# A fifth block product in sevenths: M7 of the first product, for token groups 3 to 6, and the last difference of G's parts on GpSimd

## The chip, the cores and the metric

The kernel runs on one core of a Trainium2 chip. The core has a matrix engine (TensorE, in the profile PE, with its weight loads as PEld), a vector engine (VectorE, DVE), a scalar engine (ScalarE, ACT), GpSimd (POOL) and SyncE (SP), which issues most of the DMAs. Each engine takes its own instructions in the order in which the program has them, and waits on semaphores for the others. The metric is the device time of one execution in microseconds (us), as the median of several runs; one further execution is recorded instruction by instruction, and that is the profile.

## The reference: what is computed

```python
# q, k, v: (4, 8, 768, 64); centroids: (8, 16, 64); w_in: (512, 2048); w_out: (2048, 512); all float32
mask = q_assign[:, :, :, None] == k_assign[:, :, None, :]      # nearest centroid, queries and keys
scores = np.where(mask, scale * np.matmul(q, k.transpose(0, 1, 3, 2)), -1000000000.0)
attn = softmax(scores);  attn_out = np.matmul(attn, v)
x = attn_out.transpose(0, 2, 1, 3).reshape(B * S, H * D)       # 3072 tokens x 512
h = x @ w_in                                                   # the first product
g = np.where(h > 0.0, h, np.exp(np.minimum(h, 0.0)) - 1.0)     # ELU
out = g @ w_out                                                # the second product
```

Only the two products behind the attention concern us, and of these the first one for the last four of six token groups.

## The kernel before

**Groups and blocks.** The 3072 tokens go in six groups of 512 (`k_` 0 to 5 in the code, groups 1 to 6 in this text). For each group the kernel computes the first product, transposed (2048 rows of h on the partitions, 512 tokens along them), applies ELU, and leaves the result in the buffer `g` (the tile `kq_g`); then it computes the second product from `g` and stores 512 rows of the output. All of it is float32.

**Seven block products.** Both products are cut by Winograd's form of Strassen's scheme. The weights are quartered into a11, a12, a21, a22 and the group's x into x11, x12, x21, x22; s1 to s4 and t1 to t4 are sums of these quarters. Seven products M1 = a11 x11, M2 = a12 x21, M3 = s4 x22, M4 = a22 t4, M5 = s1 t1, M6 = s2 t2, M7 = s3 t3 take the place of eight, and with U2 = M1 + M6 and U4 = U2 + M5 the quarters of h are c11 = M1 + M2, c12 = U4 + M3, c21 = U2 + M7 - M4 (the minus is in t4), c22 = U2 + M7 + M5.

**Two ways to do one of the seven.** A block product is 1024 rows by 256 tokens, with 256 to sum over. *By fourths*: the rows come in four parts (`u` 0 to 3); each part is one `block_product` (line 794), four matmuls of 128 x 128 weights with 256 columns, into one PSUM bank of 512. *In sevenths*: the same scheme is applied once more inside the block, and the block is one *unit* of seven small products m1 to m7, each of four matmuls with 128 columns. The class `InUnit` (line 1159) does that for the first product, `OutUnit` for the second. The small weight sums of a unit, where they are not blocks of the weights themselves, lie in DRAM (`far_in`) and are streamed in by SyncE, ten slots ahead (`fetch`, `weights`, `stream_of`).

**Which product is done how.** Group 1 and 2 do all seven of the first product by fourths (`unit`). In groups 3 to 6 (`FIRST_IN` = 2) the first product of a group has two stages. The first is the chain of four units M1, M6, M5, M2 (`IN_UNITS`), which runs behind the seven `OutUnit`s of the previous group's second product, in one chain (`chain`, line 1246). The second stage is `rest_of_group` (line 1326): M3, M7 and M4 by fourths, with three block products for each `u`, added in PSUM to what the chain left in `g`.

**The chain's own order.** For each unit u the chain issues m6, m2, m1 of the next unit, m7, m5 of the next unit, m3, m4; the last unit has no next one, and so only five products. A unit works in a set of four banks; two sets (`sets`) alternate from unit to unit. Between the products, ScalarE copies m1 into the bank of m6 (line 1223), m5 out to SBUF (1227), bank 2 to bank 3 (1265) and bank 3 out to SBUF (1281), and VectorE adds these in: `b2 += m5` (line 1272) must be done before m3 is accumulated into bank 2, `b4 += u3` (1284) before bank 4 is used. The four results of a unit, one per bank, are taken up by `take` (line 1198): for M1 by copies to c11, for M6 as c21 = U2, for M5 as c12 = U4 with a copy of M5 itself to c22 (line 1207, ScalarE), for M2 by adding c11 in the bank (line 1209). Results 0 and 1 are taken within the unit; 2 and 3 when the next unit's m6 has been issued, or, for the last unit, around its own m3 and at its end. The small sums of x (`xt`, line 1195) are made by GpSimd.

**ELU.** `elu_exp` (line 808) is an exponential on ScalarE from the bank into `g` (810) and a clamp on GpSimd in `g` (811); `elu` (line 813) is one VectorE instruction on `g` and the bank (814).

**The fourths.** For each `u`, `rest_of_group` does s3 t3 into bank b3, which ScalarE had filled with c21 = U2 from `g` (`begin_rest`, line 1323); VectorE makes c22 as b3 + M5 (line 1341); s4 x22 is added to b2, which had been filled with c12 = U4; a22 t4 is added to b3. Each of the three gets its ELU. Last, VectorE replaces c12 by c22 - c12 (line 1364), one of the differences that the second product needs of G's parts, one `u` later (`behind`, `flush_all`). At the head of the stage stand the four ELUs of c11 (`ready`, from the banks of the unit M2), in the order of banks 2, 0, 1, 3: all four exponentials before anything else on ScalarE, all four VectorE parts after the first block product.

**Tables in group 2.** While group 2's first product runs by fourths, VectorE makes the weight sums for the streams, four instructions to a block (`table_block` for w_out, `in_table_steps` for w_in), in steps that `fill_table` hands out two at a time; SyncE stores them (`keep_far`). The sums s2, s3, s4 of w_in were made by GpSimd in group 1 (`w_step`), and stored by GpSimd's DMAs into `s2_far` and `w_far`.

Of the kernel before, what the change touches and what calls it, by code (L numbers as in the profile page):

```python
# [9 lines left out]
F32 = mybir.dt.float32  # L10
# [9 lines left out]
P = 128  # L20
# [41 lines left out]
def main_path(ctx, tc, c, q, k, v, centroids, moe_w_in, moe_w_out, out):  # L62
# [675 lines left out]
    def x_parts(k_):  # L738
        a, b_ = slice(GS * k_, GS * k_ + QS), slice(GS * k_ + QS, GS * (k_ + 1))
        return X[:, :2, a], X[:, :2, b_], X[:, 2:, a], X[:, 2:, b_]  # L740
# [18 lines left out]
    w_far = [[far.tile([P, 512], F32, name=f"w_far{u}{n}") for n in range(2)] for u in range(4)]  # L759
    s2_far = far.tile([P, 2, 2, 512], F32, name="s2_far")  # L760

    def w_far_of(u, n):

        if n == 0:
            return s2_far[:, u // 2, :, ts(u % 2, QS)]
        return w_far[u][n - 1].rearrange("p (c n) -> p c n", c=2)

    def w_step(k_, u, n):

# [36 lines left out]
    def as_part(bank, part):  # L806
        return bank.rearrange("p (f n) -> p f n", f=part.shape[1])
# [134 lines left out]
    def table_block(a, at):  # L942


        s3, s2, s4 = (x.rearrange("p (f m) -> p f m", m=P) for x in at)
        q11, q12, q21, q22 = (part_w(a, i, j) for i in range(2) for j in range(2))
        nc.vector.tensor_tensor(s3, q11, q21, op=Alu.subtract)
        yield
        nc.vector.tensor_tensor(q21, q21, q22, op=Alu.add)
        keep_far()  # L950
        yield
        nc.vector.tensor_tensor(s2, q21, q11, op=Alu.subtract)
        yield
# [16 lines left out]
    def thirds(x):  # L970
        return [x[:, ts(m, 512)] for m in range(3)]
# [14 lines left out]
    def table_last(n):  # L986
# [9 lines left out]
        if n == 1:  # L996
            parts = [("s3", s3), ("s2", s2), ("s4", s4)]
            here["a22"].update(parts)
            made.extend((flat_far("a22", x), y) for x, y in parts)

    def table_rest():
        for n in range(4):
            nc.sync.dma_start(dead[n], s2_far[:, n // 2, n % 2])
        for a, at in (
            ("s4", thirds(s_all)),
            ("a11", thirds(p_out)),
            ("a12", thirds(s_all)),
        ):
            yield from table_block(a, at)
        yield from in_table_steps()  # L1010
# [12 lines left out]
    far_in = {  # L1023
        (a, x): far.tile([P, 512], F32, name=f"far_in_{a}_{x}")
        for _, a in IN_UNITS
        for x in (("s1", "s2", "s3", "s4") if a == "s2" else ("s2", "s3", "s4"))
    }
    for i, j, x in ((0, 0, "q11"), (0, 1, "q12"), (1, 1, "q22")):
        far_in["s2", x] = s2_far[:, i, j]

    def in_table_steps():

        for a, s1, at in (
            ("s2", dead[2], p_out),
            ("a11", dead[0], s_all),
            ("s1", dead[0], p_out),
            ("a12", dead[0], s_all),
        ):
            s3, s2, s4 = thirds(at)
            if a == "s2":  # L1040
                q11, q12, q21, q22 = dead
            else:
                q11, q12, q21, q22 = (part_in(a, i, j) for i in range(2) for j in range(2))
            nc.vector.tensor_tensor(s3, q11, q21, op=Alu.subtract)
            yield
            nc.vector.tensor_tensor(s1, q21, q22, op=Alu.add)
            keep_far()
            yield
            nc.vector.tensor_tensor(s2, s1, q11, op=Alu.subtract)
            yield  # L1050
            nc.vector.tensor_tensor(s4, q12, s2, op=Alu.subtract)
            made.extend((far_in[a, x], y) for x, y in (("s3", s3), ("s2", s2), ("s4", s4)))
            if a == "s2":
                made.append((far_in[a, "s1"], s1))
            yield
        keep_far()

    def in_place(n):
        a = ("a11", "s1", "a12")[n]
# [98 lines left out]
    class InUnit:  # L1158
        of, width = "in", 512

        def __init__(self, k_, n):
            self.k_, self.n, self.a = k_, n, IN_UNITS[n][1]
            x11, _, x21, _ = x_parts(k_)
            self.b = (x11, x_s[1], x_s[0], x21)[n]
            self.banks = banks_of(k_, n)
# [31 lines left out]
        def take(self, q_):  # L1197
            bank = self.banks[q_]
            c11, c12, c21, c22 = (part_g(b, q_ // 2, q_ % 2) for b in ("b11", "b12", "b21", "b22"))
            b = as_part(bank, c11)  # L1200
            if self.n == 0:
                nc.scalar.copy(c11, b)
            elif self.n == 1:
                nc.vector.tensor_tensor(c21, b, c11, op=Alu.add)
            elif self.n == 2:
                nc.vector.tensor_tensor(c12, b, c21, op=Alu.add)
                nc.scalar.copy(c22, b)
            else:
                nc.vector.tensor_tensor(b, b, c11, op=Alu.add)

# [3 lines left out]
        def note(self, at):  # L1214
            if at == "m4" and self.n == 2:
                rest_load(1)
            elif at == "m7" and self.n == 3:
                for n in (2, 1):
                    begin_rest(self.k_, 0, n)

    def seven_first(u):
        u.product("m1")
# [82 lines left out]
            u.take(2)  # L1305
            u.taken()

    REST = [(1, 2), (0, 3)]

    def rest_places(u):  # L1310

        return [w_tmp[:, n] if n < 3 else o_rest for n in REST[u % 2]]

    def rest_load(u):
        for n, place in enumerate(rest_places(u)):
            nc.sync.dma_start(place, w_far_of(u, n + 1))

    def begin_rest(k_, u, n):

        part = g[:, 2 * u : 2 * u + 2, QS:]  # L1320
        if n == 2:
            part = g[:, FC // 2 + 2 * u : FC // 2 + 2 * u + 2, :QS]
        nc.scalar.copy(as_part(sets[(k_ + u) % 2][n], part), part)
# [114 lines left out]

    def w_sums(k_):
        for n in range(3):  # L1440
            if n or k_ < FIRST_IN:
                w_step(k_, 0, n)

    def next_group(k_):
# [122 lines left out]
            scale_x(last_n, e_of)  # L1567
    second_product_first(early_on)

    table = table_rest()  # L1570

    def fill_table():
        next(table, None)
        next(table, None)

    for k_ in range(1, N // GS):
        if k_ < FIRST_IN:
# [269 lines left out]
```

## Time and profile before

| | us |
|---|---|
| median of 3 runs (lowest, highest) | 889.41 (888.82, 889.57) |
| the profiled execution: its own time | 889.5 |
| its span, first to last instruction | 887.7 |
| attention and group 1's first product | 0 to about 382 |
| group 1's second product | about 382 to 429.5 |
| group 2's first product | 429.5 to 478 |
| group 2's second product, with the first unit of group 3 begun in it | 478 to about 522 |
| group 3: last of the chain's units ends, and the fourths begin | 547.34 |
| group 3: the fourths end, and the second product begins | 568.06 |
| group 4, 5, 6: the fourths begin | 637.1, 726.9, 816.7 |
| TensorE, VectorE, ScalarE, GpSimd busy | 876.6, 710.7, 447.0, 227.3 |

The span is what the trace covers; the run's own time has 1.8 us more around it. In the trace, TensorE's float32 matmuls come as two records each, so that one small product of four matmuls is "x8". The duration shown for a matmul is modelled and overlaps the next one; the start times give the real pace. For VectorE and ScalarE too, the next instruction starts a little before the one ahead has ended, so a queue's pace is read from its starts. In the timeline, the bracket at the end of a line gives how long the engine was idle before and which instruction ended that.

### The profile page before, as it was taken

The numbers are of one execution on the slowest core, as the hardware profiler recorded it, in microseconds if no ns is written. First come the engines' busy times: TensorE is split into PE (matmuls) and PEld (weight loads), VectorE is DVE, ScalarE is ACT, GpSimd is POOL, SyncE is SP. The second block draws the span as 40 slices with busy tenths as digits, with TensorE's granted clock in tenths as the row PEclk, the third lists the DMA queues.
The fourth block names the chain that finished last, engine by engine and source line by source line (L and its number), as shares of the span: only waits on it lengthen the run. The fifth ranks groups of instructions, "written<-read, shape, count | busy, mean of one in ns | idle before, by whom it ended". The sixth has DMA issues, their size and how long they took to land.

```text
span 887.7 us, 17035 instructions
## 1 busy us (share of the span) xinstructions
PE 876.6 (99%) x6437; PEld 677.6 (76%) x6441; DVE 710.7 (80%) x1041; ACT 447.0 (50%) x853; POOL 227.3 (26%) x293
## 2 busy tenths in 40 slices
PE   8999999999999999999999999999999999999997
PEld 5444444444444448899989999999999999999997
DVE  4789998999988997897688957884788568956784
ACT  6667786787868754412243235422642364225421
POOL 0011121121113555841323013511351035102300
PEclk9999999999999999999999999999999999999999
DMA  7766685366337441165677876286618661876172
GB/s 219 185 127 175 158 181 121 123 125 159 84 107 217 129 141 62 59 148 151 206 249 245 276 212 178 52 279 207 188 48 265 217 191 42 267 205 205 49 231 82
DMA packets 157369, 145.68 MB, mean 164 GB/s; under 512 B 89824, under 2 KB 109280, under 8 KB 156256
## 3 DMA queue, kind: packets, MB, share of 16 engines
q1 hardware_dynamic: 151584, 132.45, 51.0%
q0 software_dynamic: 5408, 11.54, 5.7%
q8 instruction: 53, 0.87, 0.4%
q10 hardware_dynamic: 288, 0.52, 0.2%
q14 instruction: 36, 0.29, 0.1%
HBM read 114.59 MB, written 21.50 MB: 153 GB/s over the span
## 4 chain that ended last, share of the span: by engine, by line
PE 92%; POOL 3%; issue 2%; DVE 1%; DMA 1%; ACT 0%; SPq 0%; POOLq 0%; ACTq 0%
PE bank L1087 23%; PE o_bank L548 15%; PE banks L510 14%; PE bank L797 12%; PE bank L1177 9%; PE o_bank L1087 4%; PE banks L523 3%; PE o_bank L797 2%; PE d_bank L1087 2%; PE o_bank L1177 2%; PE d_bank L568 1%; PE d_bank L438 1%; POOL kq_g L811 1%; PE d_bank L1177 1%; PE banks L616 1%
## 5 line engine op out<-in xcount | busy, mean ns | idle before, releaser
L532 ACT ACTIVATE p_out<-banks 128x768 f32<-128x768 f32 x192 | 154.1, 811 | 25.2 <-PE banks L523 24.2
L548 PE MATMUL o_bank<-p_out,kq_g 128*64 128x384 f32 x768 | 130.9, 490 | 0.7 <-DMA kq_g<-in_v_dram 0.7
L548 PEld LDWEIGHTS o_bank<-p_out,kq_g 128*64 128x64 f32 x768 | 52.3, 137 | 75.5 <-issue 69.8
L811 POOL TENSOR_SCALAR kq_g<-kq_g 128x512 f32<-128x512 f32 x96 | 69.0, 728 | 109.7 <-ACT kq_g L810 108.3
L535 DVE TENSOR_TENSOR sums_w<-p_out 128x1536 f32<-128x1536 f32 x32 | 59.1, 1846 | 10.1 <-ACT p_out L532 10.1
L810 ACT ACTIVATE kq_g<-bank 128x512 f32<-128x512 f32 x68 | 39.8, 602 | 38.5 <-PE bank L797 18.4
L797 PE MATMUL bank<-xT,spare 128*128 128x256 f32 x256 | 59.2, 379 | 0.0
L540 DVE TENSOR_TENSOR sums_w<-sums_w,p_out 128x1536 f32<-128x1536 f32 x32 | 56.2, 1757 | 3.3 <-DVE sums_w L535 0.5
L609 POOL DMA_DIRECT2D sums_w<-xT x28 | 17.7, 649 | 154.3 <-DVE xT L585 92.0
L1087 PE MATMUL bank<-w_out,kq_g 128*128 128x128 f32 x448 | 56.0, 275 | 0.3 <-DVE kq_g L814 0.3
L1087 PEld LDWEIGHTS bank<-w_out,kq_g 128*128 128x128 f32 x448 | 53.4, 192 | 0.8 <-DVE kq_g L814 0.5
L797 PEld LDWEIGHTS bank<-xT,spare 128*128 128x128 f32 x256 | 48.3, 190 | 6.4
L797 PE MATMUL bank<-x_sum,w_in 128*128 128x256 f32 x224 | 52.9, 379 | 0.0
L814 DVE SCALAR_TENSOR_TENSOR kq_g<-kq_g,bank 128x512 f32<-128x512 f32 x68 | 44.9, 679 | 7.7 <-POOL kq_g L811 7.7
L797 PEld LDWEIGHTS bank<-x_sum,w_in 128*128 128x128 f32 x224 | 42.6, 190 | 5.8
L1195 POOL TENSOR_TENSOR spare<-x_sum 128x128 f32<-128x128 f32 x16 | 7.3, 457 | 154.4 <-PE bank L1177 88.8
L1391 DVE TENSOR_TENSOR kq_g<-kq_g 128x1024 f32<-128x1024 f32 x36 | 43.8, 1219 | 0.0
L562 ACT ACTIVATE xT<-o_bank 128x384 f32<-128x384 f32 x32 | 15.6, 489 | 53.8 <-PE o_bank L548 53.8
L604 POOL TENSOR_TENSOR xT<-xT,sums_w 128x384 f32<-128x384 f32 x32 | 41.1, 1305 | 1.6 <-DMA sums_w<-xT 1.6
L510 PE MATMUL banks<-x_sum,xT 64*128 64x384 f32 x192 | 39.8, 492 | 0.0
L510 PE MATMUL banks<-kq_g,xT 64*128 64x384 f32 x192 | 39.6, 491 | 0.0
L510 PE MATMUL banks<-x_sum,kq_g 64*128 64x384 f32 x192 | 39.6, 491 | 0.0
(379 smaller groups left out, 2026.6 us busy)
## 6 DMA issues: line engine op xcount, KB each, us to landing
kq_g<-in_v_dram SPq DMA_DIRECT2D x32, 384.0 KB, 3.7
sums_w<-far_s_s SPq DMA_DIRECT2D x42, 256.0 KB, 3.7
spare<-w_far SPq DMA_DIRECT2D x32, 256.0 KB, 3.0
words_w<-far_s_s SPq DMA_DIRECT2D x26, 256.0 KB, 3.2
out_dram<-p_out SPq DMA_DIRECT2D x22, 256.0 KB, 3.3
w_out<-in_q_dram SPq DMA_DIRECT2D x112, 48.0 KB, 2.6
sums_w<-xT POOLq DMA_DIRECT2D x28, 192.0 KB, 3.2
sums_w<-far_s_q SPq DMA_DIRECT2D x21, 256.0 KB, 3.6
```

Of the source, the lines that this page charges most:

```text
L510: nc.tensor.matmul(s[:, e, :HS], lhsT=kT[b % 2][pr][rows, ts(kt, P)], rhs=qT[half][pr][rows], start=True, stop=False,)
L532: nc.scalar.activation(probs[kt], s[:, :, :HS], Act.Exp, scale=SCALE)
L535: nc.vector.tensor_tensor(add_to, probs_all[:, : 4 * HS], probs_all[:, 4 * HS : 8 * HS], op=Alu.add)
L540: nc.vector.tensor_tensor(add_to, add_to, probs_all[:, 8 * HS :], op=Alu.add)
L548: nc.tensor.matmul(o_bank[64 * e : 64 * e + 64, :HS], lhsT=v_raw[n % 2][:, e, kt], rhs=probs[kt][:, e], start=(kt == 0), stop=(kt == NT - 1),)
L604: nc.gpsimd.tensor_tensor(x_of(n), x_of(n), r, op=Alu.mult)
L797: nc.tensor.matmul(bank[:, ts(f, QS)], lhsT=left[:, ch, ts(f, P)], rhs=right[:, ch], start=first and f == 0 and ch == 0, stop=ch == 1, ski ...
L811: nc.gpsimd.tensor_scalar(to, to, 1.0, 0.0, op0=Alu.min, op1=Alu.max)
L814: nc.vector.scalar_tensor_tensor(to, to, -1.0, as_part(bank, to), op0=Alu.add, op1=Alu.max)
L1087: nc.tensor.matmul(bank[:, :P], lhsT=left[:, f], rhs=right[:, f], start=first and f == 0, stop=last and f == 3, skip_group_check=True,)
L1177: nc.tensor.matmul(bank[:, ts(f, P)], lhsT=left[:, ts(f, P)], rhs=right, start=m in ("m1", "m5") and f == 0, stop=True, skip_group_check=True,
L1391: nc.vector.tensor_tensor(b[to][:, f], b[x][:, f], b[y][:, f], op=op)
```

## The change

In groups 3 to 6, M7 moves from the fourths into the chain, as a fifth unit between M5 and M2. Its four results are taken by two VectorE instructions each: c21 = U2 + M7 in `g`, and c22 = M7 + U4 in the bank. c22 gets its ELU from that bank, in steps that `note` puts behind products of the units M7 and M2 (`fourths`); M5 is no longer copied to c22. The first two fills of b2 and b3 for the fourths (`begin_rest`) move into the same steps. The fourths keep two block products for each `u`, s4 x22 and a22 t4. The difference c22 - c12 goes from VectorE to GpSimd. The set of banks for each unit is renumbered, since the chain has twelve units now instead of eleven.

The s3 sums of w_in get one array in DRAM, `s3_far`, in the form that `s2_far` has, and a table of their own: in group 2, VectorE makes four more sums (block "s3"), SyncE loads four pieces of `s3_far` for them and stores four results. The table's blocks are put in another order, and `fill_table` hands out three steps in each of its first four calls. Of the weight sums for the fourths, s4 alone is loaded.

```diff
-    IN_UNITS = [("M1", "a11"), ("M6", "s2"), ("M5", "s1"), ("M2", "a12")]
+    IN_UNITS = [("M1", "a11"), ("M6", "s2"), ("M5", "s1"), ("M7", "s3"), ("M2", "a12")]
...
     def banks_of(k_, n):
-        return sets[(k_ + n) % 2]
+        return sets[(min(k_, 1) + n) % 2]
...
             elif self.n == 2:
                 nc.vector.tensor_tensor(c12, b, c21, op=Alu.add)
-                nc.scalar.copy(c22, b)
+            elif self.n == 3:
+                nc.vector.tensor_tensor(c21, b, c21, op=Alu.add)
+                nc.vector.tensor_tensor(b, b, c12, op=Alu.add)
             else:
                 nc.vector.tensor_tensor(b, b, c11, op=Alu.add)
...
         def note(self, at):
             if at == "m4" and self.n == 2:
                 rest_load(1)
-            elif at == "m7" and self.n == 3:
-                for n in (2, 1):
-                    begin_rest(self.k_, 0, n)
+
+            fourths = [(part_g("b22", q_ // 2, q_ % 2), sets[1][q_]) for q_ in range(4)]
+            step = {(3, "m7"): 0, (3, "m4"): 1, (4, "m2"): 2, (4, "m7"): 3, (4, "m4"): 4}
+            n = step.get((self.n, at))
+            if n is None:
+                return
+            if n < 4:
+                elu_exp(*fourths[n])
+            if n == 3:
+                begin_rest(self.k_, 0, 1)
+            if n > 0:
+                elu(*fourths[n - 1])
+            if n == 4:
+                begin_rest(self.k_, 0, 2)
...
     def rest_of_group(k_):
-        _, t3, _, x22 = x_parts(k_)
-        t4 = x_s[2]
-        ready = [(part_g("b11", q_ // 2, q_ % 2), banks_of(k_, 3)[q_]) for q_ in (2, 0, 1, 3)]
+        x22, t4 = x_parts(k_)[3], x_s[2]
+        ready = [(part_g("b11", q_ // 2, q_ % 2), sets[0][q_]) for q_ in (2, 0, 1, 3)]
         for part, bank in ready:
             elu_exp(part, bank)
         for u in range(4):
-            _, b2, b3, b4 = sets[(k_ + u) % 2]
-            s3, s4 = rest_places(u)
+            _, b2, b3, _ = sets[(1 + u) % 2]
...
-            block_product(b3, s3, t3, False)
-            nc.vector.tensor_tensor(as_part(b4, c22), as_part(b3, c22), c22, op=Alu.add)
+            block_product(b2, rest_place(u), x22, False)
             if u > 0:
                 flush_all()
-            if u == 0:
+            else:
                 for part, bank in ready:
                     elu(part, bank)
-            block_product(b2, s4, x22, False)
             if u < 2:
                 rest_load(u + 2)
-            elu_exp(c22, b4)
+            elu_exp(c12, b2)
             if u < 3:
-                begin_rest(k_, u + 1, 2)
+                for n in (1, 2):
+                    begin_rest(k_, u + 1, n)
             for t in {1: ("t1",), 2: ("t2",), 3: ("t3", "t4")}.get(u, ()):
                 t_step(0, t)
-            elu_exp(c12, b2)
-            if u < 3:
-                begin_rest(k_, u + 1, 1)
-            elu(c22, b4)
             block_product(b3, a22, t4, False)
             elu_exp(c21, b3)
             elu(c12, b2)
 
             def rest(c12=c12, c21=c21, c22=c22, b3=b3):
-                nc.vector.tensor_tensor(c12, c22, c12, op=Alu.subtract)
+                nc.gpsimd.tensor_tensor(c12, c22, c12, op=Alu.subtract)
                 elu(c21, b3)
...
     def table_rest():
...
+        scratch = p_out[:, 1536:2048]
+        yield from table_block("s4", thirds(s_all))
+        yield from table_block("a11", thirds(p_out))
+        yield from in_table_block("s2", dead[2], s_all)
+        yield from table_block("a12", thirds(p_out))
+        to_dead(s3_far)
+        yield from in_table_block("a11", scratch, s_all)
+        yield from in_table_block("s1", scratch, p_out)
+        yield from in_table_block("s3", dead[2], s_all)
+        yield from in_table_block("a12", scratch, p_out)
+        keep_far()
...
     def fill_table():
-        next(table, None)
-        next(table, None)
+        nonlocal filled
+        filled += 1
+        for _ in range(3 if filled <= 4 else 2):
+            next(table, None)
```

More of the change, by code (lines that the diff above doesn't have):

```diff
@@ L757, in w_parts @@
         return w_in[:, :2, low], w_in[:, 2:, low], w_in[:, :2, high], w_in[:, 2:, high]
-    w_far = [[far.tile([P, 512], F32, name=f"w_far{u}{n}") for n in range(2)] for u in range(4)]
     s2_far = far.tile([P, 2, 2, 512], F32, name="s2_far")
+    s3_far = far.tile([P, 2, 2, 512], F32, name="s3_far")
+    s4_far = [far.tile([P, 512], F32, name=f"s4_far{u}") for u in range(4)]
     def w_far_of(u, n):
-        if n == 0:
-            return s2_far[:, u // 2, :, ts(u % 2, QS)]
-        return w_far[u][n - 1].rearrange("p (c n) -> p c n", c=2)
+        if n < 2:
+            return (s2_far, s3_far)[n][:, u // 2, :, ts(u % 2, QS)]
+        return s4_far[u].rearrange("p (c n) -> p c n", c=2)
     def w_step(k_, u, n):
@@ L999, in table_last, with to_dead @@
             made.extend((flat_far("a22", x), y) for x, y in parts)
+    def to_dead(x):
+        for n in range(4):
+            nc.sync.dma_start(dead[n], x[:, n // 2, n % 2])
     def table_rest():
[L1002 to L1010, printed above, removed]
+        scratch = p_out[:, 1536:2048]
[9 more added lines that the diff above has]
+        keep_far()
     WHICH = {"m1": "q11", "m2": "q12", "m3": "s4", "m4": "q22", "m5": "s1", "m6": "s2", "m7": "s3"}
     HERE = {"m1": (0, 0), "m2": (0, 1), "m4": (1, 1), "m5": (1, 0)}
-    IN_UNITS = [("M1", "a11"), ("M6", "s2"), ("M5", "s1"), ("M2", "a12")]
+    IN_UNITS = [("M1", "a11"), ("M6", "s2"), ("M5", "s1"), ("M7", "s3"), ("M2", "a12")]
     FIRST_IN = 2
@@ L1025, in main_path @@
         for _, a in IN_UNITS
-        for x in (("s1", "s2", "s3", "s4") if a == "s2" else ("s2", "s3", "s4"))
+        for x in (("s1", "s2", "s3", "s4") if a in ("s2", "s3") else ("s2", "s3", "s4"))
     }
@@ L1029, in main_path, with in_table_block @@
         far_in["s2", x] = s2_far[:, i, j]
[L1031 to L1055, printed above, removed]
-        keep_far()
+        far_in["s3", x] = s3_far[:, i, j]
+    def in_table_block(a, s1, at):
+        s3, s2, s4 = thirds(at)
+        if a in ("s2", "s3"):
+            q11, q12, q21, q22 = dead
+        else:
+            q11, q12, q21, q22 = (part_in(a, i, j) for i in range(2) for j in range(2))
+        nc.vector.tensor_tensor(s3, q11, q21, op=Alu.subtract)
+        yield
+        nc.vector.tensor_tensor(s1, q21, q22, op=Alu.add)
+        keep_far()
+        yield
+        nc.vector.tensor_tensor(s2, s1, q11, op=Alu.subtract)
+        yield
+        nc.vector.tensor_tensor(s4, q12, s2, op=Alu.subtract)
+        made.extend((far_in[a, x], y) for x, y in (("s3", s3), ("s2", s2), ("s4", s4)))
+        if a in ("s2", "s3"):
+            made.append((far_in[a, "s1"], s1))
+        yield
     def in_place(n):
@@ L1162, in __init__ @@
             self.k_, self.n, self.a = k_, n, IN_UNITS[n][1]
-            x11, _, x21, _ = x_parts(k_)
-            self.b = (x11, x_s[1], x_s[0], x21)[n]
-            self.banks = banks_of(k_, n)
+            x11, t3, x21, _ = x_parts(k_)
+            self.b = (x11, x_s[1], x_s[0], t3, x21)[n]
+            self.banks = sets[n % 2]
             self.m5 = o_flat[:, 1536:] if n % 2 else stage[:, 1]
@@ L1306, in chain, with rest_place @@
             u.taken()
-    REST = [(1, 2), (0, 3)]
-    def rest_places(u):
-        return [w_tmp[:, n] if n < 3 else o_rest for n in REST[u % 2]]
+    def rest_place(u):
+        return w_tmp[:, 2 - 2 * (u % 2)]
     def rest_load(u):
-        for n, place in enumerate(rest_places(u)):
-            nc.sync.dma_start(place, w_far_of(u, n + 1))
+        nc.sync.dma_start(rest_place(u), w_far_of(u, 2))
     def begin_rest(k_, u, n):
@@ L1322, in begin_rest @@
             part = g[:, FC // 2 + 2 * u : FC // 2 + 2 * u + 2, :QS]
-        nc.scalar.copy(as_part(sets[(k_ + u) % 2][n], part), part)
+        nc.scalar.copy(as_part(sets[(1 + u) % 2][n], part), part)
     def rest_of_group(k_):
-        _, t3, _, x22 = x_parts(k_)
-        t4 = x_s[2]
-        ready = [(part_g("b11", q_ // 2, q_ % 2), banks_of(k_, 3)[q_]) for q_ in (2, 0, 1, 3)]
+        x22, t4 = x_parts(k_)[3], x_s[2]
+        ready = [(part_g("b11", q_ // 2, q_ % 2), sets[0][q_]) for q_ in (2, 0, 1, 3)]
         for part, bank in ready:
@@ L1338, in rest_of_group @@
             c12, c21, c22 = g[:, low, QS:], g[:, high, :QS], g[:, high, QS:]
-            block_product(b3, s3, t3, False)
-            nc.vector.tensor_tensor(as_part(b4, c22), as_part(b3, c22), c22, op=Alu.add)
+            block_product(b2, rest_place(u), x22, False)
             if u > 0:
                 flush_all()
-            if u == 0:
+            else:
                 for part, bank in ready:
                     elu(part, bank)
-            block_product(b2, s4, x22, False)
             if u < 2:
                 rest_load(u + 2)
-            elu_exp(c22, b4)
+            elu_exp(c12, b2)
             if u < 3:
-                begin_rest(k_, u + 1, 2)
+                for n in (1, 2):
+                    begin_rest(k_, u + 1, n)
             for t in {1: ("t1",), 2: ("t2",), 3: ("t3", "t4")}.get(u, ()):
                 t_step(0, t)
-            elu_exp(c12, b2)
-            if u < 3:
-                begin_rest(k_, u + 1, 1)
-            elu(c22, b4)
             block_product(b3, a22, t4, False)
@@ L1440, in w_sums @@
         for n in range(3):
-            if n or k_ < FIRST_IN:
+            if n == 2 or k_ < FIRST_IN:
                 w_step(k_, 0, n)
@@ L1568, in main_path @@
     second_product_first(early_on)
+    to_dead(s2_far)
     table = table_rest()
+    filled = 0
     def fill_table():
-        next(table, None)
-        next(table, None)
+        nonlocal filled
+        filled += 1
+        for _ in range(3 if filled <= 4 else 2):
+            next(table, None)
     for k_ in range(1, N // GS):
```

## The prediction, made before the changed kernel had run

> **What bounds the kernel now.** I read the page first (busy time by engine), then the busy time of the two stages concerned, then the chain of waits for TensorE's pace, then the timeline of group 3's last unit and first fourths.
>
> ```profile
> span 887.7 us, 17035 instructions
> PE 876.6 (99%) x6437; PEld 677.6 (76%) x6441; DVE 710.7 (80%) x1041; ACT 447.0 (50%) x853; POOL 227.3 (26%) x293
> ```
>
> ```profile
> core 0: us, PE busy (x) PEld busy (x) DVE busy (x) ACT busy (x) POOL busy (x), PEclk, DMA share, GB/s
> 519.40:547.34 27.94, 27.94 (x251) 27.82 (x249) 13.29 (x25) 14.71 (x27) 5.40 (x12) 1.00 0.74 223
> 547.34:568.06 20.72, 20.72 (x98) 18.24 (x97) 16.88 (x27) 11.21 (x21) 9.07 (x15) 1.00 0.25 71
> ```
>
> TensorE has no gap in either stage of group 3 (chain, then fourths). VectorE is at 13.29 of 27.94 us in the chain and at 16.88 of 20.72 in the fourths: it has room in both, but as an average.
>
> ```profile
> 524.01 3.57 PE bank L1177 x32
> 547.50 6.91 PE bank L797 x32
> ```
>
> The chain of waits gives TensorE's pace: a small product (x8) takes 0.893 us, a block product of a fourth (x8) 1.727. Twelve of the latter make 20.72, the whole stage.
>
> ```profile
> 542.80 1.29 DVE L1206 TENSOR_TENSOR kq_g<-bank,kq_g 128x512 f32<-128x512 f32 x2 [0.20 <-PE bank L1177]
> 544.36 0.70 DVE L1272 TENSOR_TENSOR o_bank<-o_bank,p_out 128x512 f32<-128x512 f32 x1 [0.26 <-ACT bank L1265]
> 544.96 0.69 DVE L1209 TENSOR_TENSOR bank<-bank,kq_g 128x512 f32<-128x512 f32 x1
> 545.39 1.06 PE L1177 MATMUL o_bank<-xT,sums_w 128*128 128x128 f32 x8
> 546.37 1.13 PE L1177 MATMUL bank<-spare,w_in 128*128 128x128 f32 x8
> 547.34 3.62 PE L797 MATMUL bank<-xT,spare 128*128 128x256 f32 x16
> 548.20 0.69 DVE L1209 TENSOR_TENSOR bank<-bank,kq_g 128x512 f32<-128x512 f32 x1
> 548.92 1.09 ACT L810 ACTIVATE kq_g<-bank 128x512 f32<-128x512 f32 x2 [1.68 <-DVE bank L1209]
> 549.61 3.57 POOL L811 TENSOR_SCALAR kq_g<-kq_g 128x512 f32<-128x512 f32 x6 [6.23 <-ACT kq_g L810]
> 551.46 0.68 DVE L814 SCALAR_TENSOR_TENSOR kq_g<-kq_g,o_bank 128x512 f32<-128x512 f32 x1
> 552.33 0.64 ACT L1323 COPY o_bank<-kq_g 128x512 f32<-128x512 f32 x1
> 554.25 1.89 PE L797 MATMUL o_bank<-xT,p_out 128*128 128x256 f32 x8
> 569.52 1.27 POOL L747 TENSOR_TENSOR x_sum<-xT 128x512 f32<-128x512 f32 x1
> ```
>
> Two thin margins. VectorE's `b2 += m5` of the last unit (544.36, ended 545.06) frees m3 at 545.39: 0.33 us to spare. The last result of the chain is taken at 548.20, 1.55 us after TensorE has gone on to the fourths; only then do the four c11 exponentials start on ScalarE (548.92), and behind them stand the copies that fill the banks of `u` = 1. The later of these ends at 552.97, TensorE needs it at 554.25.
>
> [...] ScalarE is idle 1.68 us ahead of 548.92 for one late add with all else behind it. [...]
>
> **The change, part by part.** All times are on group 3's clock of before.
>
> *TensorE.* Four block products (4 x 1.727 = 6.91) become seven small ones (7 x 0.893 = 6.25): -0.65 us a group.
>
> *VectorE in the chain.* Everything up to the unit M5 stays. The new unit M7 stands where M2 stood: m6 at 542.60, then m2, m1 of M2, m7, m5 of M2, m3, m4 every 0.893, so m7 at 545.28, m3 at 547.07; M2's m6, m2, m7, m3, m4 at 548.86, 549.75, 550.64, 551.54, 552.43, and the fourths could begin at 553.32. A result can be read 1.10 us after its product starts (product 534.56, VectorE 535.66). VectorE, by the built order, 0.61 apart where nothing is awaited:
> - 544.36 `b2 += m5`; 544.97 and 545.58 result 0, twice; 547.00 `b4 += u3` (m7 + 1.10 + 0.62 for ScalarE's copy); 548.17 and 548.78 result 1, twice (m3 + 1.10).
> - From here there is no gap: ELU of fourth 0 at 549.39, results 2 and 3 in four instructions from 550.00, and only then M2's `b2 += m5` at 552.44, ended 553.14. M2's m3 wanted it at 551.54. **TensorE stops for 1.65 us.** Queued behind it are m4 and the fourths.
> - Then result 0, ELU 1, `b4 += u3`, ELU 2, results 3 and 1, ELU 3, and result 2 at 557.3, ended 558.0.
>
> TensorE meanwhile does m3, m4 and the two products of `u` = 0 from 555.0 to 558.5; their fills (554.4 and 555.6 on ScalarE, after ELU 1 and 2) are just in time.
>
> *The release of `u` = 1.* ScalarE's first c11 exponential, bank 2, waits for that last result: 558.03. From the first exponential to the ELU of bank 1 it took 548.92 to 551.46 before, 2.54 us, with the same queue order; so 560.57, ended 561.25. Bank 1 is the one that b2 of `u` = 1 needs filled: copy 561.3 to 561.9, product at 562.0. Without any stop TensorE would be there at 553.32 + 2 x 1.727 = 556.77. So 5.2 us are lost, in two pieces of 1.65 and about 3.5; the second would absorb the first, since VectorE's queue, not TensorE, sets 562.0. Before, the stage with three products a fourth (5.18 us) covered this; with two (3.45) it does not.
>
> *From `u` = 1 on.* Each fourth has 3.45 us. ScalarE has four instructions (2.0), VectorE two and a t sum (2.0), GpSimd two clamps of 0.6 and the difference, for which I take L747's 1.27 (up to 1.6 in L749): 2.5 to 2.8. Fills end about 0.4 us before TensorE wants them. Moving the difference costs nothing here; were GpSimd to need over 3.45, the excess would be paid three times a group. The fourths end at 562.0 + 6 x 1.727 = 572.36, against 568.06 before: **+4.3 us a group** (-0.65, +5.2, and 0.27 that the old last unit lost in spacing is inside the stop now). Four groups: +17.2.
>
> *DMA.* A group streams seven pieces of 256 KB more and loads four fewer. The unit M6 already streams seven in 6.25 us with no wait of TensorE: nothing.
>
> *Group 1.* GpSimd's store of s3 now has the form of s2's, whose issue is 0.74 us against 0.59 in this stage: 4 x 0.15 on GpSimd, and TensorE waits only 0.3 + 0.3 near that stage's end. I take 0.2 (0 to 0.6).
>
> *Group 2.* Four more VectorE sums, 3.0 us (a block ran 448.67 to 451.73), all in `u` = 0, where twelve steps are handed out instead of eight. VectorE had 0.51 + 1.10 idle there, so the next `b2 += m5` moves from 448.06 to about 449.6, ended 450.3; its product comes at 450.66. Hidden by 0.3 us; should a sum wait for a store that still reads its place, or the four loads from `s3_far` hold SyncE's queue, up to 2. I take 0.
>
> Sum against the profiled execution: 889.5 + 17.2 + 0.2 = 906.9. That execution is 0.1 above the median shown, so 906.8.
>
> **Rivals.** *A, faster:* VectorE's queue is not late, and the TensorE work decides: 889.4 - 4 x 0.65 = 886.8. For it: VectorE is only half busy in the chain. Against: it needs M2's `b2 += m5` at 550.8 and result 2 some 5 us earlier, that is a pace under 0.4 us where the trace never shows less than 0.59. *B, only the first stop counts:* the fills of `u` = 1 come in time, for instance because ScalarE passes the c11 exponentials before result 2 is late: 1.65 - 0.65 - 0.27 = 0.7 a group, 892.4. Against: the queue order. *C, more than I count:* [...] TensorE stops again at `u` = 2 and 3 (1 to 1.5 us a group), and group 2 loses 2: 906.8 + 6 = 913. For it: the margins of 0.3 to 0.4 us; two-input work of GpSimd here takes 1.27 to 2.79 us (L780). *D:* the work moves but the end is set elsewhere: excluded, TensorE is 99% busy and sets the end.
>
> **How the numbers follow.** My forecast 0.78, A 0.05, B 0.07, C 0.10. The forecast's own range: 0.5 us a group less (VectorE at 0.59, ScalarE's and GpSimd's steps 0.1 shorter) or 0.8 more (clamps at 0.75 us, copies at 0.64) gives 904.6 to 910. Wider, with part of B and of C: 901 to 911. This kernel's measurement tells about 0.2%, 1.8 us, from no change. Faster by more than that: A, 0.05. Within: 0.02, a B with little left of it. Slower: 0.93.
>
> **What would show it.** Right: in each of groups 3 to 6 two TensorE gaps, one of 1 to 2 us before m3 of the last unit, put down to VectorE's add at the line of `b2 += m5`, and one of 3 to 4 us before the first product of `u` = 1, put down to ScalarE's fill; VectorE without idle from the second result 1 of M7 to the end of M2; eight block products a group. Wrong: no such gaps (A), the first alone (B), gaps at `u` = 2 and 3 or in group 2 (C).

## The result, and the profile after

| | before | after |
|---|---|---|
| median (lowest, highest), us | 889.04 (887.37, 889.57), 6 runs | 915.00 (912.05, 920.14), 6 runs |
| ratio, 95% interval | | 1.0301 [1.028, 1.0323] |
| profiled execution: its own time, its span, us | 889.5, 887.7 | 914.98, 913.2 |

The change costs 26 us, 3%. The forecast was 906.8, with a range of 901 to 911: the sign is right, the time lies above the range. The page after, its first lines:

```profile
span 913.2 us, 17384 instructions
PE 883.6 (97%) x6533; PEld 683.6 (75%) x6537; DVE 721.5 (79%) x1053; ACT 449.2 (49%) x853; POOL 259.3 (28%) x325
```

TensorE was busy 99% of the span before, and is at 97% now. Its busy time has grown, by 7.0 us, although its work has become less by 4 x 0.65 us: some of the same matmuls must have become slower. Both things stand in the timeline of TensorE after; here is the end of group 3's chain, with the first fourths:

```profile
553.43 1.13 PE L1178 MATMUL bank<-spare,sums_w 128*128 128x128 f32 x8
555.80 1.16 PE L1178 MATMUL bank<-xT,sums_w 128*128 128x128 f32 x8 [1.23 <-DVE bank L1286]
556.79 1.06 PE L1178 MATMUL bank<-spare,w_in 128*128 128x128 f32 x8
557.69 1.91 PE L798 MATMUL o_bank<-xT,spare 128*128 128x256 f32 x8
559.43 1.89 PE L798 MATMUL bank<-x_sum,w_in 128*128 128x256 f32 x8
564.45 2.47 PE L798 MATMUL bank<-xT,spare 128*128 128x256 f32 x8 [3.13 <-ACT bank L1334]
566.71 3.15 PE L798 MATMUL bank<-x_sum,w_in 128*128 128x256 f32 x8
569.69 1.89 PE L798 MATMUL o_bank<-xT,spare 128*128 128x256 f32 x8
```

The two forecast gaps are there: 1.23 us before m3 of M2, for VectorE's `b2 += m5` (L1286), and 3.13 us before the first product of `u` = 1, for ScalarE's fill (L1334 is the copy in `begin_rest`). Read the start times behind the second gap: 564.45, 566.71, 569.69. Those two products took 2.26 and 2.98 us where one takes 1.727. The busy time by stretch (columns: stretch, its length, busy us of PE, PEld, DVE, ACT and POOL with the number of instructions, granted clock, DMA share, GB/s) tells why:

```profile
562.00:564.40 2.40, 0.00 (x0) 0.00 (x0) 2.40 (x5) 1.71 (x5) 2.16 (x4) 1.00 0.01 3
565.00:565.82 0.82, 0.82 (x5) 0.74 (x4) 0.00 (x0) 0.44 (x1) 0.30 (x1) 1.00 0.00 0
565.84:569.24 3.40, 3.40 (x9) 2.70 (x8) 2.44 (x3) 1.60 (x3) 2.23 (x3) 0.50 0.27 77
569.25:572.00 2.75, 2.75 (x14) 2.43 (x13) 0.72 (x2) 0.92 (x2) 1.37 (x2) 1.00 0.00 0
```

TensorE comes out of the gap at full clock; 1.4 us later the granted clock falls to 0.50, and 3.4 us after that it is back at 1.00. In groups 4 to 6 the same two products take 2.30 + 2.94, 2.35 + 2.90 and 2.39 + 2.85 us.

A second stop that was not forecast is in group 2, ahead of the groups that the change is for (TensorE's timeline after):

```profile
448.10 1.97 PE L798 MATMUL bank<-x_sum,spare 128*128 128x256 f32 x8 [2.18 <-DMA spare<-s_far]
449.90 1.89 PE L798 MATMUL bank<-xT,w_in 128*128 128x256 f32 x8
```

The sum, on the profiled executions. The first product of `u` = 1 starts at 564.45, 660.07, 755.68 and 851.30 us, a period of 95.62; the groups were 89.77 apart before. That is +5.85 a group:

| part, per group | us |
|---|---|
| TensorE work | -0.65 |
| lost spacing in the old last unit, now gone | -0.27 |
| first stop: 2.37 from start to start, less the 0.89 of a product | +1.48 |
| second stop: 5.02, less 1.73 | +3.29 |
| the two products behind it, less what they take after an ordinary gap (e1 below: 1.84 + 1.73) | +1.67 |
| small spacings, the rest | +0.3 |

Four groups make +23.4. Group 2's first product takes 2.41 longer, from the wait above. Group 1 ends 0.28 later. That is 26.1, against 25.5 between the spans; the missing 0.6 is gained behind TensorE's last product (it starts at 880.26 before and 906.33 after), and I haven't traced it further.

### The profile page after: what moved, and what is told of

The parts are those of the page before. It is cut to its first block, busy times and chain, and to the rows that moved or that the text cites. A ratio compares the mean times of both kernels' runs of the same rounds, so it can differ in the third digit from the quotient of the medians.

```text
span 913.2 us, 17384 instructions
## 1 busy us (share of the span) xinstructions
PE 883.6 (97%) x6533; PEld 683.6 (75%) x6537; DVE 721.5 (79%) x1053; ACT 449.2 (49%) x853; POOL 259.3 (28%) x325
## 4 chain that ended last, share of the span: by engine, by line
PE 85%; DVE 6%; POOL 3%; issue 2%; DMA 1%; SPq 1%; ACT 1%; POOLq 0%; ACTq 0%
PE bank L1088 22%; PE o_bank L548 14%; PE banks L510 14%; PE bank L1178 9%; PE bank L798 9%; PE o_bank L1088 4%; PE banks L523 3%; PE d_bank L1088 2%; DVE kq_g L815 2%; PE o_bank L1178 2%; PE o_bank L798 2%; PE d_bank L568 1%; POOL kq_g L812 1%; PE d_bank L438 1%; DVE bank L1212 1%
## 5 line engine op out<-in xcount | busy, mean ns | idle before, releaser
L812 POOL TENSOR_SCALAR kq_g<-kq_g 128x512 f32<-128x512 f32 x96 | 72.0, 759 | 98.2 <-ACT kq_g L811 97.9
L815 DVE SCALAR_TENSOR_TENSOR kq_g<-kq_g,bank 128x512 f32<-128x512 f32 x72 | 47.8, 681 | 27.2 <-POOL kq_g L812 26.9
L798 PE MATMUL bank<-x_sum,w_in 128*128 128x256 f32 x224 | 57.7, 404 | 0.0
L798 PEld LDWEIGHTS bank<-x_sum,w_in 128*128 128x128 f32 x224 | 46.6, 208 | 7.6
L798 PE MATMUL bank<-xT,spare 128*128 128x256 f32 x160 | 39.7, 397 | 12.5 <-ACT bank L1334 12.5
L798 PEld LDWEIGHTS bank<-xT,spare 128*128 128x128 f32 x160 | 30.8, 194 | 18.2 <-ACT bank L1334 14.1
L1384 DVE TENSOR_TENSOR p_out<-kq_g,p_out 128x512 f32<-128x512 f32 x35 | 28.4, 810 | 16.7 <-PE bank L1088 16.2
```

The costliest lines, as they stand in the source:

```text
L798: nc.tensor.matmul(bank[:, ts(f, QS)], lhsT=left[:, ch, ts(f, P)], rhs=right[:, ch], start=first and f == 0 and ch == 0, stop=ch == 1, ski ...
L812: nc.gpsimd.tensor_scalar(to, to, 1.0, 0.0, op0=Alu.min, op1=Alu.max)
L815: nc.vector.scalar_tensor_tensor(to, to, -1.0, as_part(bank, to), op0=Alu.add, op1=Alu.max)
```

## The experiments

All compare with the kernel before on the same chip; its median there was 888.6 to 888.7.

### Does the order of ScalarE's exponentials set the second stop? (e1)

```diff
-        ready = [(part_g("b11", q_ // 2, q_ % 2), sets[0][q_]) for q_ in (2, 0, 1, 3)]
+        ready = [(part_g("b11", q_ // 2, q_ % 2), sets[0][q_]) for q_ in (1, 0, 3, 2)]
```

Bank 1, which `u` = 1 needs first, is served first; bank 2, whose result comes last, is served last.

> The changed kernel with one line altered: the four c11 parts at the head of the fourths in the order of banks 1, 0, 3, 2 instead of 2, 0, 1, 3, so that bank 1, which the fourth u = 1 needs, is released first and bank 2, whose result is the last on VectorE, comes last. Theory (VectorE's late queue holds the first c11 exponential, so ScalarE's fill for u = 1 is late, TensorE stands idle for 3.1 us, and because it stood idle so long it runs the next two block products at a lower granted clock, 1.8 us more): the fill comes about 2.3 us earlier, the gap before u = 1 shrinks to about 0.9 us, the two products behind it take 1.73 us each at clock 1.00; 4 x (2.3 + 1.8) = 16 us less, about 899 us. Rival (the two products are slow because VectorE and GpSimd read the same memory while they run): they stay at 2.3 and 3.0 us, only 9 us are gained, about 906 us.

Measured: 901.67 (899.03 to 902.20), ratio 1.0136 [1.0119, 1.0152]. TensorE's timeline in e1:

```profile
557.98 1.16 PE L1178 MATMUL bank<-xT,sums_w 128*128 128x128 f32 x8 [1.23 <-DVE bank L1286]
...
564.64 1.99 PE L798 MATMUL bank<-xT,spare 128*128 128x256 f32 x8 [1.14 <-ACT bank L1334]
566.48 1.89 PE L798 MATMUL bank<-x_sum,w_in 128*128 128x256 f32 x8
568.20 1.89 PE L798 MATMUL o_bank<-xT,spare 128*128 128x256 f32 x8
```

The second gap falls from 3.13 to 1.14 us, and with it the slow products: 1.84 and 1.73. One group is 91.95 long (m3 at 557.98 and 649.93), 3.67 less than after: 1.99 from the gap and 1.67 from the two products. So the release behind bank 2 is the cause of the larger part of the second stop (1.14 us are left), and an order of four items is worth 13 us. The 902 is higher than the expectation for two reasons: a group gained 3.67 us and not 4.1, and group 2's gap was 2.44 us in e1, with two products behind it of 2.59 and 2.63 us, 1.7 us more than after's.

### Is the first stop paid beside the second? (e2)

```diff
             if i > 0:
                 units[i - 1].take(2)
+                if early:
+                    nc.vector.tensor_tensor(b2, b2, u.m5, op=Alu.add)
                 units[i - 1].take(3)
                 units[i - 1].taken()
...
-            nc.vector.tensor_tensor(b2, b2, u.m5, op=Alu.add)
+            if not early:
+                nc.vector.tensor_tensor(b2, b2, u.m5, op=Alu.add)
```

`early` is the unit M2 in groups 3 to 6.

> The changed kernel with VectorE's b2 += m5 of the unit M2 put ahead of the two instructions on result 3 of M7, 1.2 us earlier in VectorE's queue. Theory (VectorE's backlog as a whole sets when u = 1 is released; the stop before m3 is absorbed): the stop before m3 falls from 1.2 us to nearly nothing, TensorE stops instead before the first fourth, whose fill comes no earlier, and the time is the same, 915 within 1.5 us. Rival (each stop is paid by itself): 4 x 1.2 us less, about 910 us.

Measured: 914.03 (911.82 to 916.90), ratio 1.0294. TensorE's largest waits in e2 (total us, times, longest):

```profile
PE bank L798 <- ACT bank L1338: 12.5, 4, 3.1
PE o_bank L798 <- ACT o_bank L1338: 3.8, 4, 1.0
PE bank L798 <- DMA spare<-s_far: 2.3, 1, 2.3
```

No wait before m3 is left, and no time is gained: 0.95 us now stand before the first product of `u` = 0, and the second gap is as long as before. TensorE arrives earlier and waits for the same thing, VectorE's last result. So the first stop isn't paid beside the second: VectorE's queue sets the end of both.

### What does the slow clock cost? (e3)

```diff
             block_product(b3, a22, t4, False)
+            if u == 0:
+                for _ in range(14):
+                    nc.tensor.matmul(sets[1][3], lhsT=blank,
+                        rhs=blank[:, 0:1].to_broadcast([P, 512]), start=True, stop=True)
```

Fourteen bf16 products of zeros in the gap before `u` = 1, into a bank that isn't in use; they compute nothing. Measured, they fill 3.28 us (559.85 to 563.13 below, 13 of the 14 in the trace).

> The changed kernel with fourteen matmuls on zeros (bf16, 128 x 512[...], into a bank that is not in use) behind the second block product of u = 0, where TensorE stands idle for 3.1 us; nothing that waits is moved. Theory (idle time lowers the clock): the products behind run at 1.73 us and clock 1.00, 4 x 1.8 = 7 us less, about 908 us. Rival (contention with VectorE and GpSimd in that stretch): 2.3 and 3.0 us stay, 915 us.

Measured: 907.92 (906.50 to 909.13), ratio 1.022. TensorE in e3:

```profile
559.85 3.21 PE L1366 MATMUL d_bank<-blank 128*128 128x512 bf16 x13
563.13 1.99 PE L798 MATMUL bank<-xT,spare 128*128 128x256 f32 x8
564.96 1.89 PE L798 MATMUL bank<-x_sum,w_in 128*128 128x256 f32 x8
566.69 1.89 PE L798 MATMUL o_bank<-xT,spare 128*128 128x256 f32 x8
```

The product of `u` = 1 still starts 8.64 us behind m3 of M2 (554.49), as it does after (8.65); nothing starts earlier. But the next two take 1.83 and 1.73, the mean granted clock of the profiled execution is 1.000, and a group is 93.93 long: 1.69 less than after. Seven us of the change's loss are thus not waiting: they are what TensorE's idling costs in clock afterwards. And 93.93 - 89.77 = 4.16 is what the forecast had put at 4.3.

### What did group 2 wait for? (e4)

SyncE's queue in group 2, before and after (L773/774 is the load of a fourth's s2, L931/932 the stores of the table's results):

```profile
434.88 0.37 SPq L773 DMA_DIRECT2D spare<-s_far  x1
436.86 3.41 SPq L931 DMA_DIRECT2D far_s_s<-sums_w  x4
440.33 2.99 SPq L931 DMA_DIRECT2D far_s_q<-sums_w  x3
```

```profile
437.14 3.41 SPq L932 DMA_DIRECT2D far_s_s<-sums_w  x4
440.60 2.98 SPq L932 DMA_DIRECT2D far_s_q<-sums_w  x3
443.67 1.43 SPq L774 DMA_DIRECT2D spare<-s_far  x2
```

Before, the load of `u` = 1's s2 went out at 434.88, ahead of seven stores; after, at 443.67, behind them, and it had landed at about 448. In the code the load stands behind two calls of `fill`. With two steps a call, the stores of block s4 came only in the calls behind it; with three steps they are in the calls ahead of it.

```diff
         nc.vector.tensor_tensor(b2, b2, m5, op=Alu.add)
+        if u < 3 and k_ > 0:
+            w_step(k_, u + 1, 0)
         fill()
         fill()
-        if u < 3:
+        if u < 3 and k_ == 0:
             w_step(k_, u + 1, 0)
```

> The changed kernel with the load of the next fourth's s2 in group 2 issued ahead of the two calls that hand out table steps, so that on SyncE's queue it stands before the seven stores of block s4 again, as in the kernel before. Theory (that load, 8 us later on SyncE's queue than before, makes TensorE wait 2.2 us at 448): the wait goes, 915 - 2.2 = 912.8 us, the groups 3 to 6 unchanged. Rival (it waits for s2_far's or s3_far's own store in group 1, or VectorE is what is late there): the wait stays or moves to VectorE's add, 915 us.

Measured: 911.60 (910.83 to 912.30), ratio 1.026, 3.4 us less than after and more than forecast. 1.3 of it is the wait (0.85 for 2.18). In the profiled run 1.7 more come from the clock, which did not fall in group 3; what the other runs gained beyond the wait isn't traced. TensorE's waits from group 2 on in e4:

```profile
PE bank L798 <- ACT bank L1336: 12.5, 4, 3.1
PE bank L1180 <- DVE bank L1288: 4.9, 4, 1.2
PE bank L798 <- DMA spare<-s_far: 0.8, 1, 0.8
```

The wait of 2.2 us is gone, so the place behind the stores was its cause. One of 0.8 has come at 461.86, at the load of s3 for `u` = 2: on SyncE it stands behind the four loads from `s3_far`, which hold the queue from 450.07 to 454.56. That these loads make it was not tested alone; in e8 below, where they come one block later, TensorE waits for no load. In group 3 the first product behind the gap took 1.83 us, though the gap was 3.12 as in groups 4 to 6, where it took 3.43 to 3.51.

### Does the difference on GpSimd cost anything? (e5)

```diff
-                nc.gpsimd.tensor_tensor(c12, c22, c12, op=Alu.subtract)
+                nc.vector.tensor_tensor(c12, c22, c12, op=Alu.subtract)
```

> The changed kernel with the difference c22 - c12 back on VectorE. Theory (in the fourths VectorE and GpSimd both have room, so where the difference is done costs nothing): the same time, 915 within 2.5 us, and the same gaps of 1.2 and 3.1 us in each group. Rival (GpSimd's difference holds its clamps and so the release of the fourths, or slows VectorE): several us faster, 910 or below.

Measured: 915.17 (913.69 to 917.11), ratio 1.0294 [1.0278, 1.031]. The gaps are the same, 1.23 and 3.12 in each group, and groups 4 to 6 follow each other as after, at 95.6 us. It costs nothing and brings nothing here. (In e5's profiled run two products of group 2 were slow as well, 2.35 + 2.86 us, and in group 3 the two took 3.57 + 2.97, 2.97 us more than the 1.84 + 1.73 of e1; the last section takes this up.) On GpSimd in the changed kernel, the difference takes as long as the forecast had it:

```profile
566.10 1.27 POOL L1368 TENSOR_TENSOR kq_g<-kq_g 128x512 f32<-128x512 f32 x1
```

### How long must TensorE stand idle for its clock to fall? (g5, g8, g12)

In after the clock fell behind gaps of 3.13 us, and not behind those of 1.23 and 2.18. To have idling without the rest of the change, the kernel before gets n copies of a tile onto itself on ScalarE, ahead of the c11 exponentials of each of groups 3 to 6; they delay the fills of `u` = 1 and compute nothing. n is 5, 8 and 12.

```diff
+        for _ in range(8):
+            nc.scalar.copy(stage[:, 2], stage[:, 2])
         for part, bank in ready:
             elu_exp(part, bank)
```

> The kernel before with five idle copies (128 x 512 in SBUF, about 0.5 us each) on ScalarE ahead of the c11 exponentials of each of groups 3 to 6; they compute nothing. They delay the fill of u = 1 by 2.5 us where it had 0.55 to spare, so TensorE stands idle for about 2 us once a group. Theory (only a gap of about 3 us or more lowers the clock): products behind at 1.73 us, clock 1.00, 889 + 4 x 2.0 = 897 us. Rival (any stop lowers it): 2 us more a group, 904 us.

> The kernel before with eight such copies: a gap of about 3.5 us once a group. Theory: the product or two behind the gap run at about half clock and take 1.7 us more in sum, 889 + 4 x (3.5 + 1.7) = 910 us, the mean clock at about 0.99 as in the changed kernel. Rival (the clock drop belongs to the new order of work, not to the idle time): 889 + 4 x 3.5 = 903 us, clock 0.998.

> The kernel before with twelve idle copies on ScalarE in each of groups 3 to 6, in the place of g5 and g8: those made gaps of 0.7 and 2.6 us, so a copy costs 0.65 us and the first two us are free; here the gap is 5.2 us. Theory (the longer the idle time, the surer the lower clock): all four groups have it, about 1.75 us each: 888.7 + 4 x (5.2 + 0.2 + 1.75) = 917 us. Rival (the clock falls in some groups only whatever the length of the gap, as with 2.6 us, where it fell in two of four): 910 to 914.

| | median us, ratio | gap in each group | the two products behind it, groups 3 to 6 |
|---|---|---|---|
| g5 | 893.19, 1.0052 | 0.7 | 1.83 + 1.73 in group 3; clock 0.999 over the run |
| g8 | 902.32, 1.0155 | 2.64 | 2.55 + 2.69, 1.83 + 1.73, 1.83 + 1.7, 2.39 + 2.85 |
| g12 | 919.65, 1.0351 | 5.23 | 3.58 + 1.85, 3.58 + 2.76, 3.38 + 1.73, 3.58 + 2.60 |

The gaps of g5 and g8 are shorter than I had expected (2 and 3.5), since part of the copies fell into ScalarE's 1.68 us of idle time; the times are lower accordingly. g12 lies 2.7 us above its expectation; 1.8 of it is in the two products behind its gaps, which take 8.8 us more in the four groups than 1.84 + 1.73 each, for the 4 x 1.75 = 7.0 expected. g8's first gap (a copy took 0.65 us, 5.16 for eight):

```profile
546.89 5.16 ACT L1332 COPY spare<-spare 128x512 f32<-128x512 f32 x8
...
555.04 2.76 PE L797 MATMUL bank<-xT,spare 128*128 128x256 f32 x8 [2.63 <-ACT bank L1323]
557.59 2.85 PE L797 MATMUL o_bank<-xT,p_out 128*128 128x256 f32 x8
560.28 1.89 PE L797 MATMUL bank<-x_sum,w_in 128*128 128x256 f32 x8
```

So an idle stretch alone, in the unchanged kernel, brings the slow products about. At one and the same length of 2.64 us it did so in two groups of four: length isn't all that decides.

### Can the change be made to pay? (e6, e8)

e6 keeps the change and takes every cause found above away. In the last unit, `b2 += m5` comes between the two VectorE instructions of a result; the exponentials and ELUs are spread, bank 1 before the others; `u` = 1's first fill comes before the last results are in, which other banks for the fourths (`rest_banks`) allow; the load stands ahead of the fills, as in e4, and the loads from `s3_far` one block later. `fill_table` hands out two steps in each call, as before.

```diff
+    def last_in_unit(prev, u):
+        b1, b2, b3, b4 = u.banks
...
+        prev.take(2, "a")
+        nc.vector.tensor_tensor(b2, b2, u.m5, op=Alu.add)
+        prev.take(2, "b")
...
+        begin_rest(u.k_, 0, 2)
+        begin_rest(u.k_, 1, 1)
+        nc.vector.tensor_tensor(b4, b4, u.u3, op=Alu.add)
+        u.product("m3")
+        u.take(1)
...
+    def rest_banks(u):
+        one, two = sets
+        return ((two[1], two[2]), (two[0], two[3]), (one[1], one[2]), (one[0], one[3]))[u]
...
+        ready = [(part_g("b11", q_ // 2, q_ % 2), sets[0][q_]) for q_ in range(4)]
+        elu_exp(*ready[1])
...
-        for _ in range(3 if filled <= 4 else 2):
+        for _ in range(2):
```

> The changed kernel with the same work in another order. (1) For the unit M2, VectorE does b2 += m5 and the ELU of fourth 1 between the results of M7, and its own results 1 and 3 first. (2) The fourths use the banks 1, 2 and then 0, 3 of M7's set and only then those of M2's set, so that u = 1 waits for no ELU of c11; the c11 exponentials are spread behind the fills. (3) In group 2 two steps to each call, the next s2 loaded ahead of them, the loads from s3_far one block later. Theory (the work of the change is cheaper on TensorE by 0.65 us a group, and all the rest of the 26 us is waits made by queue order, the lower clock and SyncE's late load): no gap over 0.3 us in groups 3 to 6, 889.0 - 4 x 0.65 = 886.4 us, 0.3% below the kernel before; if a stop of 0.5 us a group is left, 888.5. Rival (VectorE has too much work in the units M7 and M2 for any order): gaps of 1 us or more stay in each group, 892 or above.

Measured: 891.08 (890.36 to 893.16), ratio 1.003 [1.0018, 1.0043]: a miss. No gap over 0.25 us is left in groups 3 to 6. But in group 2's second product stands a new one; TensorE and, first, the VectorE instruction that it waits for:

```profile
485.95 0.68 DVE L1420 TENSOR_TENSOR p_out<-kq_g 128x512 f32<-128x512 f32 x1
...
486.69 2.08 PE L1090 MATMUL bank<-w_out,p_out 128*128 128x128 f32 x8 [3.37 <-DVE p_out L1420]
488.56 1.91 PE L1090 MATMUL o_bank<-words_w,kq_g 128*128 128x128 f32 x8
490.26 1.91 PE L1090 MATMUL bank<-w_out,p_out 128*128 128x128 f32 x8
491.97 1.18 PE L1090 MATMUL bank<-words_w,p_out 128*128 128x128 f32 x8
```

The table has four steps more than before. At two a call they reach into the second product, where VectorE makes its sums late. And here too the stop is followed by half speed: three small products at 1.87, 1.70 and 1.71 us instead of 0.89, 2.6 us on top of 3.4. e8 is e6 with the three steps of the change put back:

```diff
-        for _ in range(2):
+        for _ in range(3 if filled <= 4 else 2):
```

> The kernel of e6_reordered, with three table steps again in each of the first four calls in group 2, as in the changed kernel. In e6 the only gap left was in group 2's second product: 3.4 us, with the three products behind it 2.6 us too long, because the table ended late and VectorE's first t sum with it. Theory (that gap is the table's): it goes, and no other comes; 891.1 - 6.0 = 885.1 us, below the kernel before's 888.7 by about 0.4%. Rival (three steps bring SyncE's late load back, 2.2 us, or the gap has another cause): 887.5 or above.

Measured: 886.59 (885.47 to 887.78, 13 runs) against 888.61 of before (17 runs), ratio 0.9979 [0.9971, 0.9987]. That is faster than before, but 1.5 us above the expectation, and why isn't traced. TensorE in e8, at the place of the two stops:

```profile
550.90 1.13 PE L1180 MATMUL bank<-spare,sums_w 128*128 128x128 f32 x8
551.86 1.06 PE L1180 MATMUL bank<-xT,sums_w 128*128 128x128 f32 x8
552.85 1.13 PE L1180 MATMUL bank<-spare,w_in 128*128 128x128 f32 x8
553.82 1.93 PE L798 MATMUL o_bank<-xT,spare 128*128 128x256 f32 x8
555.58 1.89 PE L798 MATMUL bank<-x_sum,w_in 128*128 128x256 f32 x8
557.31 1.89 PE L798 MATMUL bank<-xT,spare 128*128 128x256 f32 x8
```

No gap, and no slow product. The fourths of group 4 begin 89.22 us behind those of group 3 (643.04 and 553.82), 0.55 less than the 89.77 of before, near the 0.65 of work that the change takes off TensorE. Four times 0.55 is 2.2, and 2.0 was measured. So the idea of the change pays, by 0.2%, when VectorE's and ScalarE's queues are put in the order in which TensorE needs their results; as it was written it costs 3%.

## Why the prediction was wrong, and where it was right

**VectorE's queue, the first stop: right.** The chain of group 3 begins 2.69 us later after than before (its first product of M1 at 522.07 and 519.38). With that, the forecast has `b2 += m5` at 552.44 + 2.69 = 555.13, and m3, from the end of the add, at 555.8. VectorE's timeline after:

```profile
555.05 0.69 DVE L1286 TENSOR_TENSOR bank<-bank,spare 128x512 f32<-128x512 f32 x1
```

555.05, and m3 at 555.80. The loss against an even pace is 1.48 instead of 1.65.

**The release of `u` = 1, the second stop: right.** Forecast, with the shift: last result 560.0, first exponential 560.7, copy 564.0, product 564.7. The last result and ScalarE's two lines after it:

```profile
559.84 0.69 DVE L1212 TENSOR_TENSOR bank<-bank,kq_g 128x512 f32<-128x512 f32 x1
560.56 2.06 ACT L811 ACTIVATE kq_g<-bank 128x512 f32<-128x512 f32 x4 [1.82 <-DVE bank L1212]
563.81 1.11 ACT L1334 COPY bank<-kq_g 128x512 f32<-128x512 f32 x2 [0.69 <-DVE kq_g L815]
```

559.84, 560.56, 563.81, and the product at 564.45. That the second stop absorbs the first was shown by e2; that ScalarE's order makes 1.99 us of it, by e1. Without the clock's part, e3 has 4.16 us a group for 4.3.

**"The fourths end at 562.0 + 6 x 1.727": the step that failed.** It took TensorE's pace as fixed behind a stop of 3.5 us. The first two of the six products take 1.67 us more, 6.7 us in four groups: the larger of the two terms that the sum lacked. e3 shows it by removal (907.92), g8 and g12 by causing it in the kernel before. None of the prediction's rivals had it, so the range could not reach it. What the runs show is half speed: in each of after's groups 3 to 6 the granted clock was 0.50 for 3.41 us, and in g12 a product of 1.73 us took up to 3.58. It costs 1.65 to 1.7 us in most cases, and up to 2.97 (e5, group 3). The clock fell behind gaps from 1.91 us on, see the last section.

**"Group 2 ... Hidden by 0.3 us ... I take 0": failed as well.** It cost 2.41. I had looked at VectorE's place and at the four loads from `s3_far`. What moved was an older load, which three steps a call instead of two put behind seven stores on SyncE (e4). The order of SyncE's instructions showed it: the load's line hadn't changed, its place in the queue had. The suspect that the prediction named, the four loads, may be real too (it was not tested alone), but is worth only 0.8, and only once the first is gone.

**The smaller terms.** Group 1: +0.28 for 0.2 (0 to 0.6). The difference on GpSimd: nothing for nothing (e5). DMA for the streams of M7: no gap in that unit, as forecast. Rival A did not come, and e8 shows that its reason against it, VectorE's queue and not its load, was the right one: with another order of the same instructions 0.55 of the 0.65 arrives. Rival C had nearly the right size, 913, by luck: its 2 us in group 2 came (2.41), but there were no stops at `u` = 2 and 3 and nothing from GpSimd's difference (e5); the slow clock took their place in its sum.

The two failed terms are 6.7 + 2.4 = 9.1 us, and the forecast was short by 8.2: stops of 4.16 instead of 4.3 a group, and what is gained behind group 6, give the rest back.

## What to carry to other kernels

A short stop of TensorE is not priced by its length alone. In these runs half clock followed 2 of 4 gaps of 2.64 us and 14 of 16 of 3.1, mostly for 1.7 us each, and the shortest gap that it followed was 1.91 us: allow for it in a forecast gap of that length or more. Behind e1's two gaps of 1.23 and 1.14 us in groups 3 to 6, in the place of after's 1.23 and 3.13, it did not come. When a helper hands out more steps per call, list what each queue now has ahead of every load that did not change, DMA queues first. And when an engine is "half busy", lay its queue out by need: the same work cost 3% in one order and gained 0.2% in another.

## What the runs showed of the hardware that was not expected

The clock fell behind idle stretches of 1.91 us and more, and not behind all of them. Per gap of TensorE, read from the products behind it:

| idle, us | run and place | clock fell |
|---|---|---|
| 0.7 to 1.24 | g5, e1 (both gaps), the first gaps of after, e2, e3, e4, e5 | never |
| 1.82, 2.18, 2.34 | group 2 of e3, after, e2 | no (1.80, then 1.72 to 1.73) |
| 1.91, 2.44 | group 2 of e5, e1 | yes (2.35 + 2.86; 2.59 + 2.63) |
| 2.64 | g8, four groups | 2 of 4 |
| 3.1 | after, e2, e4, e5, four groups each | 4, 3, 3, 4 of 4 |
| 3.37 | group 2 of e6 | yes (three small products at 1.87, 1.70, 1.71) |
| 5.23 | g12, four groups | 4 of 4 |

A fixed limit on the gap can't give this order, since 1.91 fell and 2.34 did not. g8 shows both cases at one length of gap. In group 3, a stretch of 3.41 us in which TensorE works for 1.08 us is followed by one of 3.41 at half clock (first two lines); in group 4, stretches with 1.88 and 2.29 us of work follow each other at full clock (last two):

```profile
552.71:556.12 3.41, 1.08 (x5) 0.98 (x6) 2.84 (x5) 3.41 (x8) 3.38 (x6) 1.00 0.02 6
556.13:559.54 3.41, 3.41 (x10) 2.66 (x9) 2.53 (x5) 0.97 (x2) 0.97 (x3) 0.50 0.10 33
644.89:648.29 3.40, 1.88 (x9) 1.32 (x7) 0.64 (x2) 3.34 (x8) 1.29 (x3) 1.00 0.41 122
648.30:651.70 3.40, 2.29 (x11) 2.04 (x12) 3.29 (x7) 2.57 (x6) 2.84 (x5) 1.00 0.00 0
```

What decides between the two was not shown: no run moved a gap in time and left its length.

In after, the slow stretches begin at 565.83, 661.40, 756.98 and 852.55 us, 95.57 us apart, and each lasts 3.41 us. Its groups are 95.62 us apart, and all four were hit nearly alike, 2.26 + 2.98 to 2.39 + 2.85. In e6 the slow stretch was about 6.8 us long, an estimate from the granted clock: 0.91 on average from 480 to 486.6 us, 0.50 from 486.7 to 492, 0.97 from 492 to 496.

The clock also accounts for the spread of after's runs, 912.05 to 920.14 us: the mean granted clock was 0.994 in the fastest and 0.986 in the slowest, and 0.008 of 915 us is about 7.3 of the 8.1 us (an estimate from these figures). The spread is smaller in before, 887.37 to 889.57, and in e3, 906.50 to 909.13, whose profiled run has no gap over 2 us left.
